# Prologue of a spectral filter and mixer kernel reworked: compact first-stage matrices, one engine for batch 0's filter product, on-chip hand-over to stage 4, double-matrix blocks for batch 1

## Chip, cores, metric

One core of one Trainium2 chip. The metric is the device time of one execution in microseconds (us). All runs of the kernel after and of the experiments were in the fast state; of the kernel before, one, two and three runs of the last three calls were slow. The ratios leave these out; its medians are quoted as recorded, with them, which moves them by 0.2 us at most. A time is the median of a kernel's runs. A ratio is the mean time of one kernel's fast runs over that of the kernel before in the same rounds on the same chip, so it is not quite the ratio of the medians that are quoted; square brackets hold its 95% interval.

## The reference

```python
X = np.fft.rfft(x, axis=1)                       # x: 8 batches, 3136 tokens, 256 channels
y = np.fft.irfft(X * (filt_r + 1j * filt_i), n=3136, axis=1)
h = (y.transpose(0, 2, 1) @ U @ V).transpose(0, 2, 1)   # tokens mixed, rank 32
u = y + h
out = u + np.maximum(u @ w_ch1, 0.0) @ w_ch2     # channels mixed, 256 -> 1024 -> 256
```

## The kernel before

3136 is 64 x 49, so the transform is done in parts. Each batch goes through stage 1 (64-point transform; a 13-piece generator, written to a DRAM intermediate `ct1`), stage 2 (49-point, after loading `a2` from `ct1`), the product with the filter, stage 3 (back, written to `ct2`), the low-rank part, and stage 4 (back to tokens, after loading `e2` from `ct2`; its result is `ut`). Then come the two channel-mixing matmuls, in 52 groups of up to 512 tokens, 8 steps each. The program gives each engine one row of instructions, and a plan says in which step of the loop the parts of the *next* batches stand. In the traces below the matrix engine (PE) stands, with the rest of its row behind it, when one instruction has to wait (7.53 us in one case).

The parts that matter (cuts marked):

```python
    wf = cst.tile([128, 25, 128], F16, name="wf")         # stage-1 matrices, half of them zeros
    # ... four loads of it ...
    def st1(b):                                           # stage 1 of batch b
        # ... 12 pieces: two matmuls, one evacuation; a store after every fourth ...
        nc.sync.dma_start(dram(ct1[b], 48 * 64 * DM, [[DM, 64], [1, DM]]), al)  # small last store
        if 1 < b < NB - 1:
            load_x(b + 1, 2)                              # input of the batch after
            load_x(b + 1, 3)
        yield
    # ... mid_first(): batch 0's product, in 16 blocks
            if j in (7, 9, 12, 14):
                nc.scalar.copy(pc, pz)
                nc.gpsimd.tensor_mul(uv, pc, fin)         # four blocks on POOL
            else:
                nc.vector.tensor_mul(uv, pz, fin)
    # ...
    def make_fa(i):                                       # makes the second filter table
        s = slice(8 * i, 8 * i + 8)
        nc.scalar.copy(fc[0:64, s], fb[64:128, s])
        nc.vector.tensor_scalar_mul(fc[64:128, s], fb[64:128, s], -1.0)
        nc.vector.tensor_copy(fa[64:128, s], fb[0:64, s])
    # ... plan
    at(4, x_after, 2)
    for b in range(1, NB):
        if b == 2:
            plan_st1(b, 12, (0, 1, 3, 4, 5, 7))           # stage 1 of batch 2 from step 12
        m = later(start[b - 1], (5, -9, -12)[min(b, 3) - 1])
        z = plan_mid(b, m, (2, 5) if b > 1 else (1, 3, 5))  # blocks whose product POOL does
```

## Time and profile before

| | before |
|---|---|
| median (lowest to highest) | 557.61 us (553.35 to 560.20), 4 runs |
| span of the profiled run, mean granted clock | 555.2 us, 0.988 |
| PE busy | 93% of the span |
| first channel-mixing matmul | 61.2 us |

What bounds the kernel is read in the prediction below. Two more lines of this profile serve the comparison: the row of granted clock in 40 slices (9 is full), and the stretch from 90 to 100 us (length, then busy time of PE, its weight loads, DVE, ACT, POOL, then granted clock, DMA share, GB/s).

```profile
PEclk9999899997999999999999999999999999999999
...
90.00:100.00 10.00, 8.55 (x75) 6.12 (x73) 4.38 (x6) 8.98 (x17) 9.79 (x7) 1.00 0.79 207
```

The clock is full nearly everywhere, and at 90 to 100 us POOL is busy for almost the whole stretch. That did DVE no harm: its six operations there took 0.69 to 1.23 us each.

### The profile page before, as it was taken

How to read it: one execution, taken by the hardware profiler on the slowest of the kernel's cores; microseconds unless marked ns; L12 is line 12 of the kernel's file. 1: busy time of each engine (PE TensorE's matmuls, PEld its weight loads, DVE VectorE, ACT ScalarE, POOL GpSimd, SP SyncE). 2: the span in 40 equal slices, each digit the busy share in tenths (PEclk: the TensorE clock that was granted, in tenths of full speed). 3: DMA queues.
4: the chain of work that ended last, by engine and by line, in shares of the span. 5: the costliest groups of instructions: out<-in, count | busy, mean ns of one | idle time of the engine just before them, and what ended most of it. 6: DMA issues, size and time to landing. Idle time of an engine off the chain costs nothing.

```text
span 555.2 us, 11638 instructions
## 1 busy us (share of the span) xinstructions
PE 517.2 (93%) x4491; PEld 375.3 (68%) x4491; DVE 353.1 (64%) x409; ACT 390.8 (70%) x684; POOL 282.4 (51%) x194
## 2 busy tenths in 40 slices
PE   5976689997999999999999999999999999999996
PEld 2634356664767777777776777777786777777775
DVE  6764675755756686758846785858746887643332
ACT  8566868774777688767776788677777577765663
POOL 5778179951883165915683175806563297300000
PEclk9999899997999999999999999999999999999999
DMA  9998876894669468774879468865653553333212
GB/s 194 157 170 192 225 141 187 209 230 130 174 184 250 125 176 199 173 204 137 193 222 221 123 173 228 166 199 152 186 170 121 141 167 121 106 113 115 96 77 87
DMA packets 85432, 92.06 MB, mean 166 GB/s; under 512 B 6741, under 2 KB 69416, under 8 KB 85376
## 3 DMA queue, kind: packets, MB, share of 16 engines
q1 hardware_dynamic: 67968, 75.12, 45.5%
q0 software_dynamic: 16960, 15.91, 19.1%
q8 instruction: 35, 0.57, 0.4%
q10 hardware_dynamic: 448, 0.28, 0.3%
q14 instruction: 21, 0.17, 0.1%
HBM read 57.42 MB, written 49.77 MB: 193 GB/s over the span
## 4 chain that ended last, share of the span: by engine, by line
PE 70%; POOL 10%; DVE 7%; DMA 6%; ACT 4%; issue 2%; DVEq 0%; ACTq 0%; POOLq 0%; SPq 0%
PE psum L521 25%; PE psum L488 24%; PE psum L352 4%; PE psum L344 4%; PE psum L477 4%; PE psum L497 3%; PE psum L266 3%; POOL y L634 3%; DMA x<-in_x_dram 3%; POOL x L170 2%; DVE ut L482 1%; DVE tb L632 1%; PE psum L416 1%; DMA w1sb<-in_moe_w_ch_dram 1%; ACT asb L273 1%
## 5 line engine op out<-in xcount | busy, mean ns | idle before, releaser
L492 ACT ACTIVATE hring<-psum 128x512 f16<-128x512 f32 (+1 forms) x416 | 237.7, 576 | 104.5 <-PE psum L488 103.2
L488 PE MATMUL psum<-ut,w1sb 128*128 128x512 f16 (+1 forms) x832 | 240.3, 370 | 6.4 <-ACT hring L492 3.0
L521 PE MATMUL psum<-w2sb,hring 128*128 128x256 f16 x1536 | 230.9, 273 | 0.0
L634 POOL TENSOR_TENSOR y<-ta,tb 128x1024 f16<-128x1024 f16 x56 | 120.5, 2159 | 159.4 <-DVE tb L632 115.5
L521 PEld LDWEIGHTS <-hring 128*128 128x128 f16 x1536 | 143.3, 98 | 63.8 <-issue 3.8
L482 DVE CAST ut<-psum 128x512 f16<-128x512 f32 x96 | 71.1, 741 | 108.3 <-PE psum L477 88.2
L488 PEld LDWEIGHTS <-w1sb 128*128 128x128 f16 x832 | 104.6, 145 | 27.3 <-issue 10.4
L529 DVE COPY och<-psum 128x512 f32<-128x512 f32 x96 | 66.2, 689 | 47.3 <-PE psum L497 46.6
L326 ACT CAST esb<-psum 98x512 f16<-98x512 f32 x128 | 74.7, 586 | 21.6 <-PE psum L344 16.0
L628 DVE TENSOR_TENSOR ta<-psum,fb 128x1024 f16<-128x1024 f32 x41 | 50.0, 1218 | 7.9 <-PE psum L352 6.9
L273 ACT CAST asb<-psum 128x512 f16<-128x512 f32 x78 | 45.7, 589 | 12.3 <-PE psum L266 11.2
L497 PE MATMUL psum<-idn,ut 128*128 128x128 f16 x392 | 54.0, 220 | 0.0
L477 PEld LDWEIGHTS <-e 96*128 96x128 f16 x768 | 35.9, 99 | 25.5 <-issue 10.2
L630 DVE TENSOR_TENSOR tb<-psum,fc 64x1024 f16<-64x1024 f32 x41 | 50.3, 1226 | 0.9
L632 DVE TENSOR_TENSOR tb<-psum,fc 64x1024 f16<-64x1024 f32 x41 | 49.9, 1218 | 0.8
L477 PE MATMUL psum<-sv,e 96*128 96x64 f16 x768 | 38.8, 194 | 6.5 <-DMA e<-ct 3.7
L344 PE MATMUL psum<-y,g 128*98 128x512 f16 x105 | 39.9, 380 | 3.0 <-POOL y L634 1.5
L497 PEld LDWEIGHTS <-ut 128*128 128x128 f16 x392 | 38.4, 98 | 4.9
L628 POOL TENSOR_TENSOR ta<-pc,fb 128x1024 f16<-128x1024 f16 x15 | 32.4, 2159 | 10.7 <-ACT pc L638 10.7
L352 PE MATMUL psum<-a,w2t 98*128 98x512 f16 x113 | 34.3, 379 | 1.7 <-DVE tb L632 1.6
L266 PE MATMUL psum<-x,wf 128*128 128x256 f16 x168 | 31.3, 274 | 2.8 <-DVE asb L271 1.0
L630 POOL TENSOR_TENSOR tb<-pc,fc 64x1024 f16<-64x1024 f16 x15 | 31.8, 2122 | 1.2
(93 smaller groups left out, 373.6 us busy)
## 6 DMA issues: line engine op xcount, KB each, us to landing
out_dram<-och SPq DMA_DIRECT2D x47, 512.0 KB
ct<-esb SPq DMA_DIRECT2D x64, 196.0 KB
x<-in_x_dram POOLq DMA_DIRECT2D x48, 256.0 KB, 8.1
e<-ct SPq DMA_DIRECT2D x48, 256.0 KB
a<-ct SPq DMA_DIRECT2D x56, 196.0 KB
ct<-asb SPq DMA_DIRECT2D x42, 256.0 KB
wf<-wf SPq DMA_DIRECT2D x3, 256.0 KB
w1sb<-in_moe_w_ch_dram POOLq DMA_DIRECT2D x1, 512.0 KB, 6.8
```

The source lines that it names most:

```text
L326: nc.scalar.copy(esb[b, k][:, 2 * half:2 * half + 2, :].rearrange("p s d -> p (s d)"), pe[0:98])
L344: nc.tensor.matmul(pe[0:98], g3[:, m, :], v, start=(n == 0), stop=(n == len(parts) - 1))
L477: nc.tensor.matmul(pu[:, 64 * i:64 * i + 64], e2[b, c][:, i, 128 * dh:128 * dh + 128], sv[:, 64 * r:64 * r + 64], start=(i == 0), stop=Tru ...
L482: nc.vector.tensor_copy(o, v)
L488: nc.tensor.matmul(ph[:, 0:n], w1sb[:, dh, :, t], gr.ut[:, dh, 0:n], start=(dh == 0), stop=(dh == 1))
L492: nc.scalar.activation(h[:, 0:n], ph[:, 0:n], RELU)
L497: nc.tensor.matmul(o[:, dh * 128:dh * 128 + 128], gr.ut[:, dh, t0:t0 + n], idn, start=False, stop=(dh == 1), skip_group_check=True)
L521: nc.tensor.matmul(o, gr.h[tt][:, i * 128:(i + 1) * 128], w2sb[:, tt, :], start=(tt == 0), stop=False, skip_group_check=True)
L529: nc.vector.tensor_copy(gr.och[:, 2 * y:2 * y + 2, :].rearrange("p j d -> p (j d)"), gr.pc)
L628: eng.tensor_mul(ta, p, va)
L630: eng.tensor_mul(tb[0:64], p[64:128], vb[64:128])
L634: nc.gpsimd.tensor_add(ys[k], ta, tb)
```

## The change

Its intent is a shorter prologue:

- The stage-1 matrices are stored at half size, and DVE widens them on chip. U moves to another queue. POOL clears half of the filter table that ACT cleared before.
- Batch 0's product is done by DVE alone. Its low-rank part is spread over the blocks.
- The last eight rows that batch 0's stage 4 needs are copied from on-chip memory to on-chip memory, not stored and loaded.
- Only 8 of batch 1's 13 stage-1 pieces stay in the prologue, and the fillers there go.
- In the loop, DVE makes all of the second filter table; blocks 0, 1 and 7 of batch 1 use a double-matrix form that needs only the first table. Batch 2's input waits for batch 1's first product, so its stage 1 starts six steps later.

The core of the diff (cuts marked with `...`):

```diff
-    wf = np.zeros((128, 25, 128))
+    wf = np.zeros((128, 25, 64))
...
+    nc.gpsimd.memset(fb[32:64, 16:32], 0.0)
+    for h in range(2):
+        nc.vector.tensor_scalar_mul(wf[:, :, 64 * h:64 * h + 64], wfc[...], ...)
...
+                if k == 6:
+                    load_e2(0, 0, 56, 0)
+                if k == 7:
+                    for i in range(8):
+                        (nc.sync, nc.scalar)[i % 2].dma_start(
+                            e2[0, 0][56 + i:57 + i],
+                            esb[0, 7][49 * (i % 2):49 * (i % 2) + 8, i // 2, :])
+                    store3(0, 7)
...
+        nc.gpsimd.tensor_copy(sv[64:96, :]..., vnat...)      # V into place, ahead of w1 and x
+        nc.gpsimd.dma_start(w1sb, ...)
...
-            if j in (7, 9, 12, 14):
-                ... four products on POOL
+            uv = sb.tile([128, 2, 2 * DM], F16, tag="ta", bufs=3, name="uv")
+            nc.vector.tensor_mul(uv, pz, fin)
...
-    def make_fa(i):
-        s = slice(8 * i, 8 * i + 8)
-        nc.scalar.copy(fc[0:64, s], fb[64:128, s])
+    def make_fa(a, z):
+        s = slice(a, z)
+        nc.vector.tensor_copy(fc[0:64, s], fb[64:128, s])
...
-    keep_warm(6)
...
+                if k == 1:
+                    at(later(s, 6), make_fa, 0, 8)           # falls in step 21
...
-            load_x(b, c, groups[0].h[3] if c == 0 else None)
-    at(4, x_after, 2)
+            load_x(b, c, first_uv[0] if c == 0 else None)
+    at(12, x_after, 2)
...
-            plan_st1(b, 12, (0, 1, 3, 4, 5, 7))
+            plan_st1(b, 18, (0, 1, 3, 4, 5, 7))
...
-        m = later(start[b - 1], (5, -9, -12)[min(b, 3) - 1])
-        z = plan_mid(b, m, (2, 5) if b > 1 else (1, 3, 5))
+        m = later(start[b - 1], (9, -8, -12)[min(b, 3) - 1])
+        z = plan_mid(b, m, (2, 5) if b > 1 else (2, 4), () if b > 1 else (0, 1, 7))
```

## The prediction

> **What bounds the kernel now.** I read the page first, then a table of busy time by stretch, then the timelines of the first 80 us, then the waits of the matrix engine, then the chain of waits.
>
> ```profile
> PE 517.2 (93%) x4491; PEld 375.3 (68%) x4491; DVE 353.1 (64%) x409; ACT 390.8 (70%) x684; POOL 282.4 (51%) x194
> ...
> PE   5976689997999999999999999999999999999996
> ```
>
> PE is the bound: from the tenth slice on it is full. What is not full is the start, and that is where the change works. By stretch (columns: length, then busy time of PE, its weight loads, DVE, ACT, POOL, granted clock, DMA):
>
> ```profile
> 50.00:60.00 10.00, 6.99 (x40) 3.86 (x40) 4.96 (x7) 7.11 (x11) 4.39 (x1) 0.85 0.78 205
> 60.00:70.00 10.00, 5.65 (x46) 3.27 (x44) 8.69 (x14) 7.88 (x10) 3.16 (x6) 0.98 0.84 202
> 70.00:80.00 10.00, 7.70 (x61) 5.39 (x60) 7.98 (x11) 5.50 (x10) 6.06 (x6) 1.00 1.03 182
> ...
> 120.00:130.00 10.00, 6.37 (x71) 4.29 (x69) 5.02 (x7) 4.93 (x10) 2.12 (x1) 0.94 0.63 184
> 130.00:140.00 10.00, 9.48 (x70) 6.47 (x71) 5.91 (x7) 5.38 (x10) 2.63 (x2) 0.72 0.59 159
> ```
>
> And over a long stretch of the loop:
>
> ```profile
> 200.00:300.00 100.00, 99.09 (x873) 73.55 (x872) 68.17 (x76) 75.61 (x142) 62.08 (x40) 1.00 0.76 193
> ```
>
> From 200 us on nothing can be won but by less PE work. The holes are before about 76 us and one at 126 to 134. PE's timeline of the start:
>
> ```profile
> 38.77 0.59 PE L344 MATMUL psum<-uv,g 128*98 128x512 f16 x2 [2.46 <-POOL uv L397]
> ...
> 57.03 2.72 PE L234 MATMUL psum<-wf 128*128 128x512 f16 x6 [0.45 <-ACT al L285]
> ...
> 59.54 0.64 PE L477 MATMUL psum<-sv,e 96*128 96x64 f16 x8
> 60.99 0.39 PE L477 MATMUL psum<-sv,e 96*128 96x64 f16 x8 [0.82 <-DVE ut L482]
> 61.22 0.41 PE L488 MATMUL psum<-ut,w1sb 128*128 128x512 f16 x1
> ...
> 66.01 1.07 PE L488 MATMUL psum<-ut,w1sb 128*128 128x512 f16 x4 [1.46 <-ACT hring L492]
> ...
> 72.04 0.38 PE L488 MATMUL psum<-ut,w1sb 128*128 128x512 f16 x1 [1.62 <-DVE ut L482]
> ...
> 130.09 0.58 PE L477 MATMUL psum<-sv,e 96*128 96x64 f16 x8 [3.73 <-DMA e<-ct]
> ```
>
> The first channel-mixing matmul (L488) stands at 61.22: all before it is prologue. The POOL product of batch 0 (L397) holds PE for 2.46 us, six filler matmuls (L234) cover the wait for stage 4's input, and after 61 the loop stumbles, because ACT and DVE make the second filter table in large pieces between the activations:
>
> ```profile
> 63.58 1.89 ACT L543 COPY fc<-fb 64x2048 f16<-64x2048 f16 x1
> ...
> 66.33 1.90 ACT L543 COPY fc<-fb 64x2048 f16<-64x2048 f16 x1
> ```
>
> The last products of batch 0, on DVE and on POOL (two timelines):
>
> ```profile
> 44.98 1.23 DVE L400 TENSOR_TENSOR uv<-psum,fb 128x1024 f16<-128x1024 f32 x1 [0.81 <-PE psum L349]
> ...
> 45.26 2.12 POOL L397 TENSOR_TENSOR uv<-pc,fb 128x1024 f16<-128x1024 f16 x1 [0.76 <-ACT pc L395]
> ```
>
> [...]the ten fillers at the start took 4.45 us, 0.43 each, against 0.22 later; after the hole of 3.73 us the granted clock is 0.72. [...]Here 1024 fp32 elements from PSUM take 1.22 us, 2048 fp16 from SBUF 0.69. So [...]pieces of the filter table are cheap there. [...]the load of 256 KB for stage 4 took 3.58 us and the store before it 6.48 in a crowded stretch.[...]
>
> **The change part by part.**
>
> *Compact matrices, U on another queue.* The stage-1 matrices shrink from 819 to 411 KB; DVE widens them with two scaled copies of 1536 elements (0.69 x 1536/2048 = 0.5 us each). U leaves POOL's queue, whose issue took 0.74 us ahead of x. But U now comes as fp32 in the queue ahead of the matrices, the fillers wait for the memset at 6 us instead of starting at 3.5, and DVE's U chain (four times 1.5 us, ended at 15.9) starts behind the widening. I estimate fillers 6.0 to 10.4, U chain to about 16.5, turned stage 1 done at 21.3: the same as now (21.5). Gain 0.2.
>
> *Batch 0's product on DVE.* Now: first product at 25.09, last one on DVE ends 46.2, last POOL product 47.4, last evacuation 49.1. After: 16 products at a pitch of 1.16 us (four in a row took 4.70: (4.70 - 1.22)/3), plus one 0.69 copy between. Four transposed inputs go to ACT in the first five steps (1.01 each beside evacuations of 0.58), about 1.6 us a step there, so 1.5 us are lost. From 24.5: 24.5 + 0.7 + 16 x 1.16 + 1.5 = 45.3 at worst, 44.8 by following each bank through. So the last product ends 2.5 us earlier than POOL's does now.
>
> *Low rank spread, last frequencies on chip.* Now 13.8 us pass from the last product (47.4) to the first L488 (61.2): stage 3, evacuation, 32 low-rank matmuls (1.06), store, load, 13 pieces of stage 1 for batch 1, fillers. After: evacuation of the last at 46.0, copies issued by two queues (four each at about 0.4 us) and landed at some 50.3; the load of the other 56 rows waits for the store before last (issued 43.4, landed about 46.5), is issued at 46.9 and lands at about 50.3 too. Beside it run the rank chain on DVE (0.4 + 0.4 + 0.9, done at 48) and 8 pieces of stage 1, ACT and DVE in turn at 0.6 to 0.7, done at 50.8. Stage 4's halves go at 50.4 and 51.6 (one bank, the DVE copy of 0.73 between). First L488 at about 52.0. Gain against 61.2: 9.2 us.
>
> *Work moved into the loop.* Counted in the programs, from the first L488 on: 1,114,368 columns before, 1,122,816 after. The 8,448 more are five pieces of stage 1 (2,304) and twelve matmuls of 512 for the three double-matrix blocks. At 0.217 us per 512: +3.6 us, and PE is the bound, so all of it counts.
>
> *First steps of the loop.* Now the holes from 61.2 to 76.3 sum to 0.57 + 0.25 + 1.46 + 1.25 + 1.62 + 0.68 and smaller, 6.6 us with the stage-4 wait of 0.82, and waits for L273 up to 100 us add 1.9: 8.5. After: no 1.9 us copies on ACT; but the first group has eight activations (0.6), two stage-1 casts and the last one on ACT, 6.3 us, against 5 of PE work; and the first intermediate load of batch 1 can only be issued once seven stores have landed (about 59.5), so it lands near 62 where step 9 wants it at 60.5. I leave 4.5 us of holes. Gain 4.0.
>
> *The hole at 126.* Batch 1's middle part ends at step 41 of 48 before and after, by the schedule's own count, so the store, load, stage 4 chain begins as far ahead of its use. The double-matrix last block and the moved x loads may take 1 us of the 3.7 and of the clock loss behind it: gain 1.0.
>
> Sum: -0.2 - 9.0 (the first two are within the 9.2) + 3.6 - 4.0 - 1.0 = -10.6. The profiled run took 557.0 us, so 546.4; I say 546.5.
>
> **The rivals.**
> 1. *The hole moves.* POOL now copies V into place (6.95 us) before it issues w1, half of batch 1's x and w2. If w2 (13.6 us from issue to landing now) is issued at 41 and collides with stores and loads, the first second-layer matmul or the first piece of stage 1 in the loop waits 2 to 5 us. For it: the DMA share is 0.8 to 1.1 between 30 and 80 us.[...] Time: 549 to 552.
> 2. *DVE becomes the bound of the first group.* All of the filter table goes to DVE in pieces of about 1.15 us (three of 0.38), beside products and evacuations. For it: DVE is at 0.87 and 0.80 from 60 to 80. Against: two of five pooled products leave and three blocks need two DVE operations instead of three, so DVE's products sum to the same 18.3 us; the pieces stand in steps without a stage-4 copy. Time: 548 to 551.
> 3. *The hole at 126 goes altogether*, with its clock loss, because the last block is two products without the POOL sum. For it: the sum took 2.12 us at 121 and 4.25 at 112. Against: same end in steps, and the store of 6.48 us was DMA crowding. Time: 541 to 544.
> 4. *The prologue is not shorter*, because stage 4 still waits for the load of 56 rows (store and load in series), or the small copies are slow to issue. Time: 550 to 554.
>
> **Range and chances.** Runs of the kernel before spread from 555.1 to 560.2 by themselves, mean 558.5, so 2% off lies at about 547.3, just above my number. The rivals weigh more upward than downward; against that stands that the schedule's constants look tuned to the chip. Range 540.5 to 553; faster by over 2% 0.54, within 2% 0.44, slower 0.02.
>
> **What would show it right or wrong.** Right: batch 0's DVE products stand in one row ending near 45; the first channel-mixing matmul stands at 51 to 53; no 1.9 us ACT copies after it; PE holes in the first 25 us of the loop sum to 4 to 5 us; the loop from there to the end some 492.6 us against 494.0 now. Wrong: first channel-mixing matmul after 55 (rival 4), a wait of over 2 us for w2, x or the intermediate (rival 1), waits of PE or ACT for DVE of over 3 us in the first group (rival 2), or no wait for stage 4's load in batch 1 (rival 3).

## The result

| | before | after |
|---|---|---|
| median (lowest to highest), 4 runs each | 557.61 us (553.35 to 560.20) | 573.94 us (572.23 to 573.95) |
| ratio of fast runs | | 1.0293 [1.0212, 1.0374]: slower |
| span, mean clock of the profiled run | 555.2 us, 0.988 | 572.1 us, 0.963 |

The page of the kernel after has these lines where the page of before had those above (busy time by engine, then PE's busy tenths and clock in 40 slices of 14.3 us):

```profile
PE 523.6 (92%) x4499; PEld 376.5 (66%) x4499; DVE 371.9 (65%) x430; ACT 377.3 (66%) x674; POOL 265.7 (46%) x184
...
PE   4896795986799999999999999999999999999996
...
PEclk9796898897799999999999999999999999999999
```

Before, PE's row was full from the seventh slice on but for one dip, a 7 in the tenth. Now it dips in slice 7 (86 to 100 us) and in slices 10 and 11 (129 to 157 us, counted from 1). The clock dips with it (0.86 granted from 86 to 100 us, 0.76 from 129 to 157). The table of stretches of the kernel after says what else ran there:

```profile
50.00:60.00 10.00, 5.96 (x36) 3.36 (x35) 4.22 (x7) 3.39 (x6) 0.00 (x0) 0.50 0.47 119
...
90.00:100.00 10.00, 3.86 (x28) 2.53 (x28) 8.80 (x6) 2.69 (x6) 9.86 (x5) 0.81 0.12 22
...
120.00:130.00 10.00, 6.60 (x53) 4.84 (x53) 4.28 (x9) 6.28 (x12) 1.57 (x3) 1.00 1.01 193
130.00:140.00 10.00, 5.88 (x56) 3.51 (x56) 2.45 (x2) 2.22 (x5) 0.00 (x0) 0.66 0.56 178
```

In the first dip DVE and POOL are both full and the DMA queues almost idle: an on-chip matter. In the second the DMA share is 1.01 as it begins and every engine has room: a transfer.

Where the time went is best seen in the times at which groups of the loop begin, read as the first channel-mixing matmul of each group (the traces hold all 832 of them, two a step, so that they can be counted off). The two right columns are experiments told below.

| group | before | after | difference | fa_xlate | fa_all |
|---|---|---|---|---|---|
| 0 | 61.2 | 57.9 | -3.3 | 57.6 | 55.5 |
| 2 | 82.9 | 81.9 | -1.0 | 82.4 | 79.2 |
| 3 | 94.9 | 98.8 | +3.9 | 92.8 | 89.6 |
| 4 | 107.3 | 112.6 | +5.3 | 104.5 | 101.4 |
| 5 | 117.9 | 125.1 | +7.3 | 118.0 | 114.8 |
| 6 | 134.7 | 149.5 | +14.8 | 132.8 | 129.6 |
| 8 | 155.9 | 172.5 | +16.6 | 156.6 | 152.3 |
| 47 | 513.6 | 530.3 | +16.7 | 514.1 | 509.9 |

The prologue did get shorter, by 3.3 us. Two groups lost most of it: 4.9 us between the starts of groups 2 and 3, and 7.6 us between those of 5 and 6; the rest came in smaller parts, 2.3 us up to group 2 and 5.2 in groups 3, 4, 6 and 7. PE's timeline of the kernel after shows both holes, in brackets the idle time before a row and what ended it:

```profile
56.10 0.59 PE L515 MATMUL psum<-sv,e 96*128 96x64 f16 x8 [1.39 <-DMA e<-esb]
...
57.90 0.61 PE L526 MATMUL psum<-ut,w1sb 128*128 128x512 f16 x1
...
98.39 0.59 PE L275 MATMUL psum<-x,wf 128*128 128x256 f16 x2 [6.08 <-DVE ut L520]
...
134.12 1.01 PE L366 MATMUL psum<-a,w2t 98*128 98x512 f16 x2 [7.53 <-DMA a<-ct]
```

**The first hole.** PE stood for 6.08 us until DVE had copied stage 4's result (`ut`). DVE was late with it because of the three pieces of the filter table before it; here they are, DVE's timeline first, POOL's second:

```profile
90.46 2.08 DVE L581 COPY fc<-fb 64x2048 f16<-64x2048 f16 x1
92.55 2.51 DVE L582 TENSOR_SCALAR fc<-fb 64x2048 f16<-64x2048 f16 x1
95.09 2.49 DVE L583 COPY fb<-fb 64x2048 f16<-64x2048 f16 x1
```

```profile
89.86 4.64 POOL L670 TENSOR_TENSOR y<-ta,tb 128x1024 f16<-128x1024 f16 x2
94.47 2.56 POOL L664 TENSOR_TENSOR ta<-pc,fb 128x1024 f16<-128x1024 f16 x1
```

Such a copy takes 0.69 us by itself (at 64.30 us in the kernel before; 0.68 and 0.69 in fa32 below). Here each ends about half a microsecond after a POOL operation does: POOL's end at about 92.0 (the first of the two in one row), 94.5 and 97.0, DVE's at 92.5, 95.1 and 97.6. POOL's own, two sums and a product, took up to 2.57 us in place of 2.12. So in this trace each copy ended only behind the POOL operation that ran when it began, 2.08 to 2.51 us after its start in place of 0.69. fa32 and nopool below test this.

**The second hole.** PE stood for 7.53 us before batch 2's stage 2 (L366), waiting for its load from the intermediate. The queue of the SyncE engine in the kernel after (start, time on the queue):

```profile
120.34 2.20 SPq L295 DMA_DIRECT2D ct<-al  x1
...
131.39 1.19 SPq L329 DMA_DIRECT2D a<-ct  x3
```

The load could be issued only when the last, small store of stage 1 (L295, 32 KB) had landed, 11 us after its issue (the load's queue waited 7.8 us for it). Four input loads of batch 3, 256 KB each, were issued from 118.40 to 120.90 on POOL's queue, just ahead of it. (Group 5 holds two shorter waits besides, 2.00 and 1.64 us for `ut` copies of DVE.)

**The first load of batch 1.** A third, shorter wait has the like cause. Five pieces of batch 1's stage 1 now stand in the first three steps of the loop, so that its small last store is issued 6.4 us after the first channel-mixing matmul, where it was issued at 59.59 us, ahead of that matmul, in the kernel before. SyncE's queue, then PE:

```profile
64.28 0.96 SPq L295 DMA_DIRECT2D ct<-al  x1
67.90 1.63 SPq L329 DMA_DIRECT2D a<-ct  x4
```

```profile
70.38 0.59 PE L366 MATMUL psum<-a,w2t 98*128 98x512 f16 x2 [2.17 <-DMA a<-ct]
```

**The prologue.** The eight on-chip copies were slow to issue. In ACT's queue:

```profile
46.99 4.54 ACTq L414 DMA_DIRECT2D e<-esb  x4
```

Four issues took 4.54 us (0.63 to 0.74 us each, with gaps that I cannot explain between them) and held up ACT's evacuations behind them until 51.63. The other four took 2.83 us on SyncE's queue from 52.00, behind the load of the other 56 rows, which itself waited until 51.63 for its store. At the start DVE's widening was slow too (DVE, then POOL):

```profile
6.29 4.48 DVE L217 TENSOR_SCALAR wf<-hring 128x1536 f16<-128x1536 f16 x2 [0.21 <-DMA hring<-wf]
```

```profile
6.33 3.50 POOL L215 MEMSET fb<- 32x4096 f16 x1
```

Two operations took 4.48 us beside POOL's memset (1.15 us without it, in all_mem below). The transposes ahead of batch 0's stage 2 began at 23.25 us, against 21.47 before.

One caution on prologue times: seven more of the runs below (fa32, nopool, mid2, fa_early, fa_xlate, fa_poolf, xl_only) run the very prologue of the kernel after, and in these eight profiles the transposes began between 22.9 and 24.4 us, stage 4 between 55.13 and 57.55, and the first channel-mixing matmul between 56.9 and 59.4. A smaller difference in the prologue between two single profiles is no result.

### The profile page after: what moved, and what is told of

Read it like the earlier page. It is cut to its first block, busy times and chain, and to the rows that moved or that the text cites. A ratio compares the mean times of both kernels' runs of the same rounds, so it can differ in the third digit from the quotient of the medians.

```text
span 572.1 us, 11654 instructions
## 1 busy us (share of the span) xinstructions
PE 523.6 (92%) x4499; PEld 376.5 (66%) x4499; DVE 371.9 (65%) x430; ACT 377.3 (66%) x674; POOL 265.7 (46%) x184
## 4 chain that ended last, share of the span: by engine, by line
PE 71%; DVE 10%; DMA 6%; POOL 5%; ACT 3%; issue 3%; SPq 0%; ACTq 0%; POOLq 0%; DVEq 0%
PE psum L526 24%; PE psum L559 24%; PE psum L366 5%; PE psum L358 4%; PE psum L515 3%; PE psum L535 3%; PE psum L275 3%; DMA ct<-al 3%; POOL y L670 2%; DVE tb L668 1%; DVE ut L520 1%; DMA ct<-esb 1%; PE psum L453 1%; ACT esb L336 1%; DVE uv L693 1%
## 5 line engine op out<-in xcount | busy, mean ns | idle before, releaser
L670 POOL TENSOR_TENSOR y<-ta,tb 128x1024 f16<-128x1024 f16 x53 | 115.0, 2175 | 174.3 <-DVE tb L668 137.3
L526 PEld LDWEIGHTS <-w1sb 128*128 128x128 f16 x832 | 105.6, 146 | 24.4 <-issue 5.6
L336 ACT CAST esb<-psum 98x512 f16<-98x512 f32 x128 | 75.2, 587 | 22.8 <-PE psum L358 16.6
L664 DVE TENSOR_TENSOR ta<-psum,fb 128x1024 f16<-128x1024 f32 x39 | 47.5, 1219 | 20.0 <-PE psum L366 19.2
L666 DVE TENSOR_TENSOR tb<-psum,fc 64x1024 f16<-64x1024 f32 x39 | 47.8, 1226 | 0.9
L668 DVE TENSOR_TENSOR tb<-psum,fc 64x1024 f16<-64x1024 f32 x39 | 47.5, 1218 | 0.7
L366 PE MATMUL psum<-a,w2t 98*128 98x512 f16 x118 | 36.5, 387 | 12.1 <-DMA a<-ct 9.7
L275 PE MATMUL psum<-x,wf 128*128 128x256 f16 x168 | 34.6, 300 | 9.9 <-DVE ut L520 7.7
L358 PE MATMUL psum<-y,g 128*98 128x512 f16 x100 | 38.2, 382 | 2.2 <-ACT esb L336 1.1
L664 POOL TENSOR_TENSOR ta<-pc,fb 128x1024 f16<-128x1024 f16 x14 | 30.7, 2195 | 16.8 <-ACT pc L674 16.8
L177 POOL DMA_DIRECT2D x<-in_x_dram x48 | 30.7, 654 | 1.1 <-POOLq L820 0.8
```

The costliest lines, as they stand in the source:

```text
L336: nc.scalar.copy(esb[b, k][:, 2 * half:2 * half + 2, :].rearrange("p s d -> p (s d)"), pe[0:98])
L358: nc.tensor.matmul(pe[0:98], g3[:, m, :], v, start=(n == 0), stop=(n == len(parts) - 1))
L366: nc.tensor.matmul(pz, w, a, start=True, stop=True)
L526: nc.tensor.matmul(ph[:, 0:n], w1sb[:, dh, :, t], gr.ut[:, dh, 0:n], start=(dh == 0), stop=(dh == 1))
L664: eng.tensor_mul(ta, p, va)
L670: nc.gpsimd.tensor_add(ys[k], ta, tb)
```

## The experiments

The main theory: the two holes have separate causes, DVE's copies beside POOL's products for the first, the small store behind input loads (met late because stage 1 of batch 2 stands six steps later) for the second. Its rival: DVE, the DMA traffic or a chain that begins in the prologue sets the pace between 60 and 150 us, so a cause taken away only moves the wait. Sixteen kernels ran in four calls; the kernel before had medians of 556.76, 556.98, 556.95 and 556.03 us in them. Each text on record says for itself which theory expects what.

### First call: the kernel after with one edit

**fa32** makes the first piece of the table in step 32 in place of step 21.

```diff
-                    at(later(s, 6), make_fa, 0, 8)
+                    at(32, make_fa, 0, 8)
```

> One edit to the changed kernel: the pieces of the second filter table for frequencies 0 to 7 are made at step 32 instead of step 21. Same work, other moment: at step 21 POOL is in its pooled products (83 to 104 us), at step 32 it should be idle. Theory A (DVE's fast copies SBUF to SBUF cannot run beside a POOL operation and wait for its end): the three pieces fall from 2.08, 2.51, 2.49 us to about 0.69 each, the hole of 6.1 us before the stage-1 matmuls goes, with the clock loss behind it; 5 to 8 us faster than the changed kernel, unless the gain is swallowed by the wait for batch 2's first intermediate. Theory B (the pieces are slow by their own size or data path): they take 2 us or more at the new place too and the hole moves there; no gain.

563.75 us, ratio 1.011 [1.0073, 1.0147]. DVE's and PE's timelines of this run:

```profile
107.69 0.68 DVE L581 COPY fc<-fb 64x2048 f16<-64x2048 f16 x1
108.39 0.69 DVE L582 TENSOR_SCALAR fc<-fb 64x2048 f16<-64x2048 f16 x1
```

```profile
124.40 1.01 PE L366 MATMUL psum<-a,w2t 98*128 98x512 f16 x2 [3.83 <-DMA a<-ct]
```

The same copies take 0.68 and 0.69 us, the first hole is gone, and the time falls by 10.2 us. Part of that is the second hole, now 3.83 us in place of 7.53: the small store and the load behind it are 5.8 us apart here (114.31 and 120.15) and not 11.0, with the same input loads about them. Why was not taken apart.

**nopool** leaves the pieces in step 21, but takes POOL's products out of batch 1. Its result is wrong (relative error 0.138): batch 1's middle part then ends after batch 2's begins, by the plan's count. I argue, but did not show, that the two then use the same PSUM banks. The timing of the copies is not touched by that.

```diff
-        z = plan_mid(b, m, (2, 5) if b > 1 else (2, 4), () if b > 1 else (0, 1, 7))
+        z = plan_mid(b, m, (2, 5) if b > 1 else (), () if b > 1 else (0, 1, 7))
```

> One edit to the changed kernel: no block of batch 1 has its product on POOL; DVE makes them all (six more products of 1.22 us on DVE). The table pieces stay at step 21. If DVE's fast copies wait for POOL operations (theory A), they take about 0.69 us each here, at the same place, because POOL does only sums there, and the hole of 6.1 us shrinks to 1 to 2. If they are slow by themselves (theory B), they stay at 2 us and more. The time is not the point: batch 1's end moves from step 41 to 44, so stage 4 of batch 1 will wait longer, and the total may be the same or slower.

569.17 us, ratio 1.0218 [1.0186, 1.0251]. DVE's timeline:

```profile
91.05 0.85 DVE L581 COPY fc<-fb 64x2048 f16<-64x2048 f16 x1
91.91 0.69 DVE L582 TENSOR_SCALAR fc<-fb 64x2048 f16<-64x2048 f16 x1
```

Same copies, same step, no POOL products beside them: 0.85 and 0.69 us (the first still met the end of a POOL sum, at 91.34). With fa32 this shows the cause of the first hole to be what POOL does at the same time, and not the step or the copies as such. The time as a whole says little, as the longer schedule of batch 1 pays for it.

**mid2** lets batch 2's middle part begin six steps later, so that its load should be there. The result is wrong here too (0.099), for the like reason, also only argued: batch 2's part now ends at step 41 and batch 3's begins at 38.

```diff
-        m = later(start[b - 1], (9, -8, -12)[min(b, 3) - 1])
+        m = later(start[b - 1], (9, -2, -12)[min(b, 3) - 1])
```

> One edit to the changed kernel: the middle part of batch 2 starts 2 steps before batch 1's groups instead of 8. Theory A (the hole of 7.5 us at 126 us is PE standing in order behind a stage-2 matmul whose intermediate is not there yet, because stage 1 of batch 2 was moved six steps later and its own slack is far larger than the hole): the hole goes or falls under 2 us, stage 2 of batch 2 finds its data, 6 to 9 us faster. Theory B (PE is short of any other work there, or DMA is so full that the next load is late too): the hole stays, now before stage 4's load of batch 1, and the gain is under 3 us.

570.66 us, ratio 1.0244 [1.0191, 1.0297]. The wait for batch 2's load went, and one of 6.2 us for stage 4's load of batch 1 took its place: batch 1's last store was issued at 128.25 us, the load behind it only at 135.57, and PE, which no longer stopped earlier, came to stage 4 before it. Standing later was no cure here.

**svlate** moves POOL's copy of V behind the issue of w1, x and w2.

```diff
-        nc.gpsimd.tensor_copy(sv[64:96, :]..., vnat...)       # ahead of w1, x, w2
+        nc.gpsimd.tensor_copy(sv[64:96, :]..., vnat...)       # behind them
```

> One edit to the changed kernel: POOL issues the loads of both weight matrices and the rest of batch 1's input before it copies V into place (7.1 us), as the kernel before does. Theory A (the prologue's end waits for the crowd that these delayed loads make: the store of batch 0's last but one frequencies took 7.4 us to land and the load behind it was issued at 51.6 instead of 46.9): the store lands in 3 to 5 us, the first channel-mixing matmul stands at 54 to 55.5 instead of 57.9, and the whole is 2 to 4 us faster. Theory B (the queue of small on-chip copies sets it: four issues of 1.1 us on ACT and 0.7 on the other queue): the first channel-mixing matmul stays within 1 us of 57.9.

569.33 us, ratio 1.0217 [1.018, 1.0253]. The first channel-mixing matmul came at 56.0 in place of 57.9, stage 4's load was issued at 49.74 in place of 51.63. Holes of 6.1 and 6.8 us remained. So with the weights and inputs loaded earlier, and out of the way of the stores and loads at the end of the prologue, that is about 2 us shorter: stage 4 began at 53.7 to 54.2 in the three runs with just this prologue (svlate, fa_all, fa_all_m6), ahead of all eight of the kernel after's. The time fell by 4.6 us; what gave the rest was not taken apart.

### Second call: fa32 with one more edit, at the prologue

**fa_early** gives batch 2's input and stage 1 their steps of before.

```diff
-            load_x(b, c, first_uv[0] if c == 0 else None)
+            load_x(b, c, groups[0].h[3] if c == 0 else None)
-    at(12, x_after, 2)
+    at(4, x_after, 2)
-            plan_st1(b, 18, (0, 1, 3, 4, 5, 7))
+            plan_st1(b, 12, (0, 1, 3, 4, 5, 7))
```

> The changed kernel with the table pieces of frequencies 0 to 7 at step 32 (as in fa32, 563.7 us), and stage 1 of batch 2 back at the steps of the kernel before: from step 12 instead of 18, its input loaded from step 4 instead of 12. Theory A (the later stage 1 is what leaves batch 2's first intermediate unloaded at step 40): PE's wait for it (3.8 us in fa32, 7.5 in the changed kernel) goes, 3 to 6 us faster than fa32. Theory B (the early load of batch 2's input collides with the stores and loads that batch 1 needs at steps 2 to 10, which is why it was moved): the wait for batch 1's first intermediate, now about 2.5 us, grows by as much, and the gain is under 2 us.

565.15 us, ratio 1.0145 [1.0111, 1.018]: no gain on fa32. PE's timeline:

```profile
73.17 1.01 PE L366 MATMUL psum<-a,w2t 98*128 98x512 f16 x2 [5.09 <-DMA a<-ct]
```

The wait for batch 2's load went, as the main theory says, but with the input loads issued early PE waited 5.09 us for batch 1's first load of the intermediate, against 2.64 in fa32, and later 3.08 us for DVE. Here the rival was right: the wait moved. So the steps of before are no longer free: moving batch 2's input and stage 1 later spares batch 1's first load.

**fa_e2dram** undoes the on-chip hand-over: all 64 rows are stored and loaded.

```diff
-                if k == 6:
-                    load_e2(0, 0, 56, 0)
-                    ... eight on-chip copies ...
                     store3(0, 7)
+                    load_e2(0, 0)
```

> As fa32, but the eight small copies on chip are taken out: after the last store of batch 0 the whole of stage 4's first input is loaded from DRAM, as the kernel before does. If the on-chip copies are worth the store and load that they replace (as predicted), stage 4 starts 3 to 5 us later than in fa32 (56.1) and the total is 3 to 5 us slower. If the path is set by the store of the last but one frequencies and the crowd on DMA anyway (rival), stage 4 starts within 1.5 us of fa32 and the total is within 1.5 us.

562.60 us, ratio 1.0094 [1.0074, 1.0114], against 1.011 [1.0073, 1.0147] of fa32 in another call. Stage 4 began at 54.66 us, no later than in any of the eight runs with the copies (55.13 to 57.55). The on-chip copies gain nothing: a store and a load in series were no slower than eight small issues.

**fa_fullwf** undoes the compact matrices and U's other queue.

```diff
-    wf = np.zeros((128, 25, 64))
+    wf = np.zeros((128, 25, 128))
-        wf[h::2, 0:24] = t1[:, 24 * h:24 * h + 24]
+        wf[h::2, 0:24, 64 * h:64 * h + 64] = t1[:, 24 * h:24 * h + 24]
... and its loads, the widening, U's load as before
```

> As fa32, but the compact stage-1 matrices are undone: the wide matrices come by DMA and U comes in fp16 by POOL's queue, as in the kernel before; no widening on DVE. Theory A (DVE's chain for U starts behind the widening and ends 1.5 to 2 us later, and turned stage 1 with it: ended 23.3 us in the changed kernel against 21.5 before): turned stage 1 ends at about 21.5, the first channel-mixing matmul stands 1.5 to 2 us earlier and the total is as much faster. Theory B (the filter loads, which are now issued later again, take over as the limit): turned stage 1 ends early, but the products of batch 0 wait for filters and the total is within 1 us.

562.26 us, ratio 1.0102 [1.008, 1.0123]: no difference shown. This does not clear the compact form, as POOL's memset stayed, and now DVE's first copy of U ran into it. That copy in the kernel before, then in this run:

```profile
7.47 1.48 DVE L243 COPY hring<-hring 64x1568 f16<-64x1568 f16 x1 [1.40 <-DMA hring<-in_moe_U_dram]
```

```profile
8.05 3.59 DVE L244 COPY hring<-hring 64x1568 f16<-64x1568 f16 x1 [1.97 <-DMA hring<-in_moe_U_dram]
```

1.48 us became 3.59 in this run, whose POOL has the memset (3.50 us in the kernel after) that the kernel before lacks. all_mem below takes it away from the widening.

**fa_sv_warm** has svlate's edit and a filler matmul after each of the eight stage-1 pieces of the prologue, meant to raise the granted clock (0.50 from 50 to 60 us in the kernel after).

```diff
+        nc.tensor.matmul(psum[:, 0, :], wf[:, 0, :],
+                         wf[:, 0:4, :].rearrange("p i m -> p (i m)"), start=True, stop=True)
```

> As fa32, with both other edits of the start: POOL copies V after it has issued the weight loads (svlate: 4.6 us faster than the changed kernel), and one filler matmul of 512 columns behind each of the eight pieces of stage 1 for batch 1 ahead of the loop. In the changed kernel the granted clock was 0.50 from 50 to 60 us, where the kernel before ran six fillers. Theory A (the cold clock costs the first group 1.5 to 2 us): first group's matmuls of 512 take 0.22 us apart from the start instead of 0.43, total 555 to 558. Theory B (ACT paces the first group anyway, fillers only delay): no gain over the two edits' sum, 558.5 to 560.

562.97 us, ratio 1.0101 [1.0077, 1.0124]: no gain. Group 0 became shorter (7.1 us, against 7.7 in fa32), and PE then waited 3.34 us for batch 1's first load. Against fa_all below, which has the same prologue but for the fillers, group 0 took 1.1 us less and began 1.5 later (56.95 against 55.46): as far as two profiles can tell, the fillers cost what they gave.

### Third call: fa32 with an edit for the second hole

**fa_xlate** takes all but the first part of batch 3's input loads out of stage 1 of batch 2 and puts them at steps 49 and 52, after the last store; batch 3's stage 1 begins eight steps later.

```diff
-            if 1 < b < NB - 1 and c:
+            if 1 < b < NB - 1 and c and (b, c) != (2, 2):
-        if 1 < b < NB - 1:
+        if 2 < b < NB - 1:
+    for n, c in ((49, 1), (52, 2), (52, 3)):
+        at(n, load_x, 3, c)
-            plan_st1(b, later(start[b - 1], -60))
+            plan_st1(b, later(start[b - 1], -60 if b > 3 else -52), (0, 4, 7) if b > 3 else (0, 2, 4, 7))
```

> As fa32 (563.7 us), but the second and third part of batch 3's input are loaded at steps 49 and 52 instead of behind stage 1 of batch 2 (steps 34 and 35), and stage 1 of batch 3 begins 8 steps later. Theory A (the wait of 3.8 us for batch 2's first intermediate is the small last store of stage 1 taking 5.8 us to land in a crowd of input loads issued one microsecond before it): the store lands in 2 to 3 us and the wait falls to 0 to 1; 3 to 5 us faster than fa32. Theory B (the schedule itself is too late: the last piece of stage 1 is computed at step 35 and the load wants it at 36): the wait stays above 2.5 us and the gain is under 1.5 us.

557.25 us, ratio 0.9998 [0.9977, 1.0018]: level with the kernel before. SyncE's queue:

```profile
113.41 0.47 SPq L295 DMA_DIRECT2D ct<-al  x1
...
115.37 1.22 SPq L329 DMA_DIRECT2D a<-ct  x3
```

From the issue of the small store to that of the load behind it are 2.0 us, in place of the 5.8 of fa32, and PE no longer waits for this load at all. This shows the cause of what fa32 had left of the second hole; xl_only below does it for the whole. (The edit's other part, the later stage 1 of batch 3, cannot have freed the store: it stood at step 39, after it.)

**fa_poolf** leaves the input loads and issues batch 2's first three loads on POOL's queue, so that nothing on SyncE's queue stands behind them.

```diff
-        nc.sync.dma_start(t, dram(ct1[b], ...))
+        (nc.gpsimd if b == 2 and k < 3 else nc.sync).dma_start(t, dram(ct1[b], ...))
```

> As fa32, but the first three loads of batch 2's intermediates are issued by POOL's queue instead of the in-order queue that also issues the stores of batch 1. Theory A (those loads stand waiting at the head of that queue for the store before them, 3 us, and hold back the last two stores of batch 1 and with them stage 4's input): the last two stores of batch 1 are issued within 0.3 us of their evacuation (fa32: 121.4 and 122.5 for casts that ended at 118.3 and 121.2), stage 4's load of batch 1 goes out 1 to 3 us earlier than 127.95, total 1 to 3 us faster. Theory B: PE stands behind the missing intermediate anyway, so the total stays within 1 us.

565.78 us, ratio 1.0143 [1.0101, 1.0185], and a wait of 4.96 us for the load remained; it went out on POOL's queue 5.5 us after the store. So the order of SyncE's queue was not what cost. It fits that the store itself landed late, which is what fa_xlate changed.

**fa_all** joins fa32, fa_xlate, fa_poolf and svlate.

> The edits of fa32, svlate, fa_xlate and fa_poolf together. If the holes are as read, all of them shrink: total 553 to 557, level with the kernel before. If each gain is taken by the next wait, as it was with svlate on top of fa32 (563.0), the total stays at 560 to 563.

554.05 us, ratio 0.995 [0.9915, 0.9986], the lowest median of all, half a per cent below the kernel before. Its span was 551.3 us at a mean clock of 0.994. PE's longest wait in the loop was this one:

```profile
67.62 0.59 PE L367 MATMUL psum<-a,w2t 98*128 98x512 f16 x2 [1.84 <-DMA a<-ct]
```

**fa_all_m6** is fa_all with batch 2's middle part two steps later.

```diff
-        m = later(start[b - 1], (9, -8, -12)[min(b, 3) - 1])
+        m = later(start[b - 1], (9, -6, -12)[min(b, 3) - 1])
```

> As fa_all, with the middle part of batch 2 started two steps later (its end in the schedule stays step 36 of 50). If the wait for batch 2's first intermediate is still over 1 us in fa_all, 1 to 2 us faster than that; if it is gone there, the same within 1 us.

554.91 us, ratio 0.9979 [0.9954, 1.0003]: not told apart from fa_all.

### Fourth call: one cause alone, and the rest of the prologue

**xl_only** is fa_xlate's edit on the kernel after, without fa32's.

> The changed kernel with only the later loads of batch 3's input (the edit of fa_xlate, without fa32). If the collision of these loads with the last store of stage 1 makes the hole of 7.5 us by itself, that hole falls to under 1.5 us while the hole of 6.1 us before the stage-1 matmuls stays: 5 to 8 us faster than the changed kernel (573.9). If the hole of 7.5 us was a consequence of the first hole, less than 2 us.

568.35 us, ratio 1.0209 [1.0168, 1.025]. PE's timeline:

```profile
97.25 0.58 PE L275 MATMUL psum<-x,wf 128*128 128x256 f16 x2 [6.08 <-DVE ut L520]
```

The first hole stands as it was, to the hundredth. The wait for batch 2's load shrank from 7.53 to 1.85 us. SyncE's queue:

```profile
119.63 0.47 SPq L295 DMA_DIRECT2D ct<-al  x1
...
124.71 1.19 SPq L329 DMA_DIRECT2D a<-ct  x3
```

The load followed the store by 5.1 us, where it was 11.0 in the kernel after; the part of the input loads that this edit leaves was issued at 110.35 and landed at 120.91, after the store's issue. The moved loads have a price, a new wait of 2.2 us for batch 3's input at 153.93. In time, the second edit alone is worth 5.6 us (573.94 - 568.35) and on top of fa32 6.5 us (563.75 - 557.25), the first alone 10.2 and on top of the second 11.1 (568.35 - 557.25). These are medians of different calls, whose medians of the kernel before differ by up to 1.6 us; within that the effects add up. The first hole costs more than its 6.08 us. Some of the rest is clock: 0.80 granted from 90 to 100 us in xl_only and 0.86 from 100 to 110, against 1.00 and 1.00 in fa_xlate.

**all_mem** is fa_all with ACT in place of POOL clearing the filter table.

```diff
-    nc.gpsimd.memset(fb[32:64, 16:32], 0.0)
+    nc.scalar.copy(fb[32:64, 16:32].rearrange("p s (k f) -> p (s k) f", f=64),
+                   free(zero, 32, 64, 0, [[0, 16 * DM // 64], [1, 64]]))
```

> fa_all (554.0) with the memset of half the filter rows back from POOL (3.5 us, 6.3 to 9.8 us) to ACT. Theory A (the same hold as at step 21: DVE's fast scaled copies wait for the POOL operation): the two widening copies fall from 4.48 us to about 1.2, the U chain and turned stage 1 end 1.5 to 2.5 us earlier (transposes at 21 to 22 instead of 23.3), total 1 to 2.5 us faster. Theory B (the widening is slow by its strided output): it stays above 3 us, no gain.

555.28 us, ratio 0.9979 [0.996, 0.9998]: no gain on fa_all. DVE's and PE's timelines:

```profile
6.49 1.15 DVE L218 TENSOR_SCALAR wf<-hring 128x1536 f16<-128x1536 f16 x2 [0.42 <-DMA hring<-wf]
```

```profile
67.57 0.59 PE L368 MATMUL psum<-a,w2t 98*128 98x512 f16 x2 [2.18 <-DMA a<-ct]
```

The widening took 1.15 us in place of 4.48, so POOL's memset was its cause. The first channel-mixing matmul came at 54.91 us, against 55.46 in fa_all; half a microsecond is less than this prologue scatters by, and less than the intervals of the two ratios can tell. Batch 1's first stage-2 matmul stands at 67.57 against 67.62, and later this profile has a wait of 2.46 us for batch 3's input (0.7 at most in fa_all).

**all_e2d** is fa_all with fa_e2dram's edit.

> fa_all with the eight copies on chip taken out, the whole first input of stage 4 loaded from DRAM. With fa32 below it, that moved stage 4 from 56.1 to 54.7 us and the total by -1 us. Theory A (their eight issues of 0.6 to 1.1 us hold ACT and the in-order queue longer than one store and one load take once DMA is not crowded): stage 4 starts at 53 to 54 against 54.0 in fa_all, total 0 to 2 us faster. Theory B (they only lost because the store in front was held by the crowd): stage 4 starts 1 us later or more and the total is slower.

555.14 us, ratio 0.999 [0.9969, 1.001]. Stage 4 began at 53.70 us, against 54.02 in fa_all and 53.72 in fa_all_m6: again the on-chip copies bring nothing forward.

**all_best** joins fa_all, all_mem, all_e2d and a last edit that gives ACT a small copy of batch 1 (32x256), which took 2.14 us on DVE beside a POOL sum and 0.22 elsewhere.

> fa_all with all_mem's and all_e2d's edits, and the low-rank rows of batch 1's last token group copied on ACT instead of DVE. If the gains add up: 549 to 552, about 1% faster than the kernel before. If group 1's wait for batch 1's first intermediate takes them back: 553 to 554.

554.92 us, ratio 0.9986 [0.9963, 1.001]: not better than fa_all. The first stage-2 matmul of batch 1 stood at 67.53, and PE waited 1.81 us for batch 3's input.

## Why the prediction was wrong, step by step

The prediction was 546.5 us, with a range up to 553 and 2% for slower. It was slower by 2.9%. The sum that the prediction built was -10.6 us; the span grew by 16.9. (Its reading of PE's row as full from the tenth slice is off: that slice shows a 7, the hole at 126.) Of its own signs of being wrong these came: the first channel-mixing matmul after 55 (57.90), and waits of over 2 us for the intermediate (2.17 and 7.53). A wait for DVE of over 3 us came too, but in group 2 and not in the first. Term by term:

1. **Compact matrices, gain 0.2.** Wrong in sign, though all_mem shows that it cost the end nothing that could be measured: the transposes ahead of stage 2 began 1.8 us later (1.4 to 2.9 in the eight runs with this prologue). The step took DVE's widening at 0.5 us an operation and did not ask what POOL did meanwhile (all_mem: 1.15 us for two without the memset, 4.48 with it).
2. **Batch 0's product on DVE, last one at 44.8 to 45.3.** The pitch was right; the last product ended at 46.24, about as much late as the start was.
3. **Low rank spread and on-chip copies, gain 9.2 with the two before.** Mis-sized: 3.3 us. Stage 4 began at 56.10 where the step said 50.4. The "copies issued by two queues (four each at about 0.4 us)" measured 0.63 to 0.76 us each, and with the gaps 4.54 us for the four on ACT's queue; the 0.4 and the landing "at some 50.3" were the author's estimates, as the kernel before has no such copy in its trace; "the load of the other 56 rows ... is issued at 46.9" measured 51.63, as the store that it waits for was issued at about 45.8, not 43.4 (its stage 3 stands in the program behind stage 2 of the last block), and landed in a crowded stretch (DMA share 0.81 from 45 to 50 us). The granted clock was 0.50 from 50 to 60 us, against 0.85 before. Rival 4 named both halves of this, so both were seen and weighed too low. fa_e2dram and all_e2d show that the copies were worth nothing; svlate, that issuing weights and inputs behind POOL's copy of V cost about 2 us of it.
4. **Work in the loop, +3.6.** As far as can be told, right. In fa_all, which has the same extra work and no long hole, PE was busy for 439.0 us from group 0 to group 47 against 434.9 before, 4.1 more. Its idle time there fell from 17.5 to 15.5 us.
5. **First steps, gain 4.0.** The waits shrank, and the gain did not come. From group 0 to group 2 PE's idle time fell from 6.1 to 4.2 us; the prediction's own sign for this, 4 to 5 us of holes in the first 25, came true. But the loop took 24.0 us there against 21.7. Of that, 2.1 is work of term 4 (4,864 columns: five pieces and five of the twelve matmuls of 512), and about 2.2 is clock, an estimate: it was granted at 0.91 and not 1.00 over these 24.0 us, after a prologue that ended at 0.50. The step left the clock out, though the prediction had read 0.72 in the trace after a hole of 3.73 us. The first load of batch 1, "near 62 where step 9 wants it at 60.5", made PE wait 2.17 us and not 1.5.
6. **The hole at 126, gain 1.0.** This step failed outright. It counted that "batch 1's middle part ends at step 41 of 48 before and after". True, but the hole that counts afterwards is another: batch 2's stage 1 had moved from step 12 to 18, its last store came behind four input loads, and PE waited 7.53 us for batch 2's load in step 40. The step named "the moved x loads" and gave them a share of a 1 us gain. fa_xlate and xl_only show them to cost 5.6 to 6.5 us.
7. **Rival 2, DVE as the bound.** The argument against it, "the pieces stand in steps without a stage-4 copy", failed. The step summed DVE's own work at 0.38 a piece and looked at where DVE's copies stood; it did not look at what POOL does in that step. The three pieces took 7.1 us, PE waited 6.08, and with the clock and what followed it cost 10 to 11 us (fa32, nopool, xl_only).

So the large errors are 6 and 7, together 16.7 us (573.94 - 557.25): in both an operation was moved to a place where another engine or queue was busy. The error of the sum is 16.9 + 10.6 = 27.5 us; 16.7 of it are the two collisions, 5.9 the prologue (9.2 - 3.3), and the remaining 4.9 answer to the gains of 4.0 and 1.0 that did not come (the 16.7 is a difference of medians of two calls). With both collisions gone what is left is a gain of 3.3 us in the prologue against 3.6 us more work: nothing, as fa_xlate measured (0.9998).

What stays open: why the small store took 11.0 us to be followed by its load in the kernel after and 5.8 in fa32, and why ACT's four issues had gaps. Batch 1's first load is not a fixed point that swallows what the prologue gains: in all runs with this change but fa_early its matmul stands 11.8 to 12.9 us behind the first channel-mixing matmul, as the store that it waits for is computed in the loop. That the wrong results of mid2 and nopool come from shared PSUM banks is argued only.

## What to carry to other kernels

When a change moves an operation in a fixed schedule, look up what the *other* engines and queues do in the place that it moves to, and not only whether its own engine has room there. Here DVE's copies of the filter table took 2.08 to 2.51 us beside POOL's operations in place of 0.69, and the load behind a store of 32 KB went 11.0 us after it with four input loads issued just ahead, 5.1 with them moved. A single wait of PE in a full loop cost more here than its length: 6.08 us of waiting cost 10 to 11, some of it clock (0.81 granted from 90 to 100 us). So three misplaced copies of 0.69 us undid a prologue gain of 3.3 us three times over. And before a microsecond at the start of a kernel is called a gain, look at how far that start scatters between runs of the same code; here it was 2.4 us.
